# Attention and MLP on one core: first keys with 49 columns, part of the W_out split on ScalarE, one more pair rounded on GpSimd

## The chip, the cores and the metric

The kernel runs on one core of one Trainium2 chip. The metric is the device time of one execution in microseconds; the median of three runs of the kernel before is 2017.74 us (2017.72 to 2019.99). A core has TensorE (PE: matrix products; PEld is its weight load), VectorE (DVE), ScalarE (ACT), GpSimd (POOL) and SyncE (SP), which issues the loads and stores here.

## The reference

Two attentions with 49 agent vectors stand between the inputs and an MLP:

```python
a2k = softmax(scale * agents @ k.T)      # per batch: 49 x 12480, over the keys
agent_v = a2k @ v                        # 49 x 128
q2a = softmax(scale * q @ agents.T)      # 12480 x 49, over the agents
x = q2a @ agent_v                        # 12480 x 128
h = x @ w_in                             # 128 -> 2048
out = (h - tanh(h)) @ w_out              # 2048 -> 128
```

There are 4 batches, so 49,920 rows in all, everything in float32. The MLP's weights arrive as float64 and are decoded on the core from their bit patterns.

## The kernel before

**Blocks and steps.** The rows are cut into 100 blocks of 500 (the last of a batch 480). One loop in `fast` (lines 854 to 910) runs over 800 steps: a step is block `n` and one of eight pairs `i` of 128-column chunks of the 2048 hidden columns. In a step PE makes the hidden values `h` of a later step (`m1`, line 563; two steps ahead as a rule), ScalarE takes tanh and square of it (lines 573 and 578), VectorE multiplies `g = h * z` (line 583), and PE adds the pair's second product into the block's accumulator (`m2`, line 632). Two blocks form a pair of blocks with positions `pos` 0 to 15, and `w_in` is folded into the agents' values beforehand, so that `m1` multiplies the q softmax (49 wide) directly with two 49 x 2048 matrices, `awh` and `awl`.

**Two forms of the second product.** `g` is float32. In the split form GpSimd rounds it to `gh` (`high`, line 613), VectorE computes `gl = g - gh` (`low`, line 618), and PE multiplies both with W_out's rounded part `wo_h` and rest `wo_l`: six terms of two products each, 12 products. In the plain form PE multiplies `g` in float32 with `wo_f`: eight product records, and no work for GpSimd and VectorE. Positions 1, 3, 7, 8 and 9 (`PLAIN`) and all of block 0 are plain. `product` (line 828) makes `g` and, if needed, `gh`; `low(1)` in the same step makes `gl` of the step before; `out` (line 840) issues the second product of the step before.

**The start.** `phase1(0)` handles batch 0 before the loop. For each of 13 groups of eight 128-key tiles, `scores` multiplies the keys (as weights) with the agents of batches 0 and 1 side by side, 98 columns (line 273), of which the copies to SBUF (line 284) and the maxima (line 286) read only the 49 of batch 0. After each of the groups 3, 5, 7 and 9 one quarter of W_in is decoded (`load_w_in`, lines 174 to 185: one ScalarE and six VectorE instructions). `max_in` and `max_out` bring the maxima of all keys into every partition, `av` subtracts them, takes the exponential and multiplies with V (lines 344 to 380). Then come the sums, the first parts of `awh` and `awl` (line 472 to 476), and the decoding of W_out's first quarter; the other three quarters are decoded in block 0, two steps each. `split_w_out` (lines 208 to 218) makes `wo_h`, `wo_l` and `wo_f` of a quarter on GpSimd, at steps 4 and 6 (the middle quarters), 8 and 9.

**The rest.** The scores, maxima and values of batch b+1 (`phase1(b + 1)`) are jobs in a list `kq`, spread over the steps of batch b: `KS`, `VS` and `OS` say at which positions how many start (`KS`: one at position 2, two at 12). The q softmax of the next pair of blocks starts at position 2, and its scores (line 508) are issued one step on; its transposes (line 538) come at positions 11 and 15. Program order is kept on PE and GpSimd from the end of the start on, and on VectorE and ScalarE from the end of the keys on (lines 916 to 919). The order of the early loads on SP's queue is that of the list `loads` (lines 716 to 725). PSUM holds four tiles of two banks, shared by `h`, accumulators, transposes and everything else (`banks` and `misc`).

Of the kernel before, what the change touches and what calls it, by code (L numbers as in the profile page):

```python
# [12 lines left out]
F32 = mybir.dt.float32  # L13
# [11 lines left out]
A = 49  # L25
# [35 lines left out]
PLAIN = (1, 3, 7, 8, 9)  # L61
NB = dict(y=2, z=2, g=4, gh=3, gl=3)
# [40 lines left out]
class Build:  # L103
# [95 lines left out]
    def load_w_in(self, c, raw):  # L199
        tiles = (self.work.tile([128, 512], F32, tag=t, name=t, bufs=2) for t in ("de", "rem", "da", "db"))  # L200
        run(self.decode(raw, self.w_in[:, c * 512 : (c + 1) * 512], *tiles))
# [6 lines left out]
    def split_w_out(self, c):  # L208
# [4 lines left out]
        nc.gpsimd.tensor_scalar(h, w, 1.0, 0.0, ALU.mult, ALU.add)  # L213
        nc.gpsimd.tensor_tensor(l, w, h.bitcast(F32), ALU.subtract)
        nc.gpsimd.memset(self.vb[c][:, :, C : C + 1], 1.0)
        for i, t in self.wo_f.items():
            if c == i // 2:
                nc.gpsimd.tensor_scalar(t, w[:, 2 * C * (i % 2) :][:, : 2 * C], 1.0, 0.0, ALU.mult, ALU.add)

    def phase1(self, b):  # L220
# [36 lines left out]
        def scores(g):  # L257
            yield
            if g == 0:
                st["s"] = self.keep.tile([128, NG * (GT + 1) * A], F32, tag="s", name="s", bufs=1)  # L260
                if b == 0:
                    st["mxp"] = self.work.tile([128, A, 2 * NG], F32, tag="mxp", name="mxp", bufs=1)
# [7 lines left out]
            if b == 0:  # L270
                ps = self.banks("h")
                for t in range(n):
                    nc.tensor.matmul(  # L273
                        ps[:, t // 4, (t % 4) * A2 : (t % 4 + 1) * A2],
                        kt[:, t, :],
                        self.ag[:, 0:2, :],
                        start=True,
                        stop=True,
                    )
                pv = ps[:, :, : 4 * A2].rearrange("p c (t a) -> p c t a", a=A2)[:, :, :, :A]  # L280
                for c in range(-(-n // 4)):
                    m = min(4, n - 4 * c)
                    sl = slice((g * GT + 4 * c) * A, (g * GT + 4 * c + m) * A)
                    nc.scalar.copy(st["s"][:, sl].rearrange("p (t a) -> p t a", a=A), pv[:, c, :m])
                banks = -(-n // 4)
                nc.vector.tensor_reduce(
                    st["mxp"][:, :, 2 * g : 2 * g + banks].rearrange("p a c -> p c a"),
                    pv[:, :banks, : min(4, n)].rearrange("p c t a -> p c a t"),
                    axis=AX.X,
                    op=ALU.max,  # L290
                )
                if g == EARLY - 1:
                    nc.vector.tensor_reduce(
                        st["mxp"][:, :, 2 * NG - 1], st["mxp"][:, :, : 2 * EARLY], axis=AX.X, op=ALU.max
                    )
# [13 lines left out]
        def max_in():  # L309
# [3 lines left out]
            part = st["mxp"] if b else st["mxp"][:, :, 2 * EARLY :]  # L313
# [302 lines left out]
    def low(self, g, gh):  # L616
        gl = self.wtile("gl", NB["gl"])[:, : g.shape[1]].bitcast(F32R)
        self.nc.vector.tensor_tensor(gl, g, gh.bitcast(F32), ALU.subtract)  # L618
        return gl

    def m2(self, acc, i, gh, gl, wf=None):
# [7 lines left out]
        for k, (weights, g, c) in enumerate(terms):  # L629
# [55 lines left out]
    def fast(self):  # L685
# [21 lines left out]
        with ExitStack() as first:  # L707
# [15 lines left out]
            for g in range(NG):  # L723
                loads.append((self.v0, g))
# [44 lines left out]
        early = self.count()  # L769
# [5 lines left out]
        rest0 = p1[2 * NG + 3 :]  # L775
        sums = rest0.pop(0)
        q1 = q_job(1)
        next(q1)
        for _ in range(3):
            next(sums)  # L780
        next(q1)
        run(sums)
        part = rest0.pop(0)
        go(part, 3)
        go(dec[0], 3)
        run(part)
        next(q1)
        go(dec[0], 1)
        run(rest0.pop(0))
        run(dec[0])  # L790
        live = []
        kq = []
        r1, r2, done = [], [], []
# [186 lines left out]
```

## Time and profile before

| | |
|---|---|
| median of three runs | 2017.74 us |
| profiled execution: its time, its span | 2016.83 us, 2015.0 us |
| mean granted clock of TensorE | 0.997 |
| VectorE's product `g` (line 583) | 800 instructions, 1194 ns each |
| GpSimd's rounding (line 613) | 544 instructions, 1566 ns each |
| VectorE's difference (line 618) | 544 instructions, 1204 ns each |
| plain second products (line 632, from `wo_f`) | 1968 records, 578 ns each |

Times in the profile are microseconds, unless marked ns, from the span's start. A row of the timeline gives start, duration, engine, line, operation, output<-inputs, shapes and count, and in brackets the idle time of the engine before it with what ended it. A row of the windows gives, for a stretch, each engine's busy time and the number of instructions that fall into it, the granted clock of TensorE (PEclk), the mean share of the DMA engines and GB/s. A row of the groups gives count, busy time, mean of one, and idle time before. PE records of successive products overlap, since one starts while the one before it drains; the distance of their starts says more than their durations. A few per cent of the PE records are missing from the trace.

### The profile page before, as it was taken

What the parts mean: (1) busy time and instruction counts of PE and PEld (TensorE: products, weight loads), DVE (VectorE), ACT (ScalarE), POOL (GpSimd) and SP (SyncE); (2) the same over time, 40 slices, a digit from 0 to 9 for tenths busy, and PEclk for the clock granted to TensorE, in tenths of its full rate; (3) what the DMA queues carried; (4) which work ended last, traced back from release to release, by engine and by line L of the source; (5) the groups of instructions that cost most, each with busy time, mean ns of one, the idle gap of its engine ahead of it and who ended that gap; (6) DMA issues with size and microseconds to landing.
All of it is one profiled execution on the core that took longest, in us unless ns stands there. A gap on an engine that the chain in (4) does not pass through costs nothing.

```text
span 2015.0 us, 49566 instructions
## 1 busy us (share of the span) xinstructions
PE 1983.3 (98%) x20775; PEld 1464.4 (73%) x20775; DVE 1827.4 (91%) x1985; ACT 1804.1 (90%) x2044; POOL 1004.1 (50%) x709
## 2 busy tenths in 40 slices
PE   8899999999999999999999999999999999999998
PEld 7477777777677777777677777777777777777775
DVE  7899999889999998898999999889899999999997
ACT  3799989899999998899999999998999999999996
POOL 1344455555445455554454454555545546555553
PEclk9999999999999999999999999999999999999999
DMA  9322112221112222221112111221101101101100
GB/s 346 123 86 92 53 57 83 73 61 46 52 61 67 77 71 61 85 67 61 33 34 92 61 57 47 68 64 56 51 29 34 54 29 37 51 30 36 39 24 27
DMA packets 76744, 129.69 MB, mean 64 GB/s; under 512 B 5400, under 2 KB 55648, under 8 KB 76512
## 3 DMA queue, kind: packets, MB, share of 16 engines
q1 hardware_dynamic: 76512, 126.44, 19.1%
q8 instruction: 165, 2.70, 0.6%
q14 instruction: 67, 0.55, 0.1%
HBM read 81.10 MB, written 25.56 MB: 53 GB/s over the span
## 4 chain that ended last, share of the span: by engine, by line
PE 84%; ACT 9%; DVE 5%; issue 1%; DMA 0%; POOL 0%; SPq 0%; DVEq 0%; POOLq 0%
PE acc L632 49%; PE h L563 26%; ACT z L578 4%; ACT y L573 4%; DVE g L583 2%; PE misc L508 2%; PE misc L357 2%; PE pt L538 1%; PE misc L301 1%; PE h L273 1%; DVE gl L618 1%; PE misc L472 1%; ACT s L349 0%; DVE qe L524 0%; DVE s L344 0%
## 5 line engine op out<-in xcount | busy, mean ns | idle before, releaser
L613 POOL TENSOR_SCALAR gh<-g 128x1000 fp32r<-128x1000 f32 (+1 forms) x544 | 852.1, 1566 | 621.9 <-DVE g L583 578.3
L583 DVE TENSOR_TENSOR g<-h,z 128x1000 f32<-128x1000 f32 (+1 forms) x800 | 954.9, 1194 | 132.8 <-ACT z L578 121.8
L573 ACT ACTIVATE y<-h 128x1000 f32<-128x1000 f32 (+1 forms) x800 | 803.2, 1004 | 72.1 <-PE h L563 63.8
L578 ACT ACTIVATE z<-y 128x1000 f32<-128x1000 f32 (+1 forms) x800 | 831.3, 1039 | 25.4
L618 DVE TENSOR_TENSOR gl<-g,gh 128x1000 fp32r<-128x1000 f32 (+1 forms) x544 | 654.7, 1204 | 0.3
L563 PE MATMUL h<-pT,awh 49*128 49x504 f32 x1600 | 551.7, 424 | 0.0
L632 PE MATMUL acc<-g,wo_f 64*128 64x500 f32 (+1 forms) x1968 | 445.2, 578 | 0.0
L632 PE MATMUL acc<-gh,wo_l 64*128 64x500 f32 (+1 forms) x2176 | 433.0, 387 | 0.3 <-POOL gh L613 0.2
L632 PE MATMUL acc<-gh,wo_h 64*128 64x500 f32 (+1 forms) x2176 | 432.7, 386 | 0.0
L563 PE MATMUL h<-pT,awl 49*128 49x504 f32 x800 | 368.7, 461 | 10.3 <-DVE g L583 4.6
L632 PE MATMUL acc<-gl,wo_h 64*128 64x500 f32 (+1 forms) x2176 | 340.9, 387 | 1.0 <-DVE gl L618 0.5
L563 PE MATMUL h<-pb,awh 49*128 49x504 f32 x1600 | 317.4, 387 | 0.0
L563 PE MATMUL h<-pb,awl 49*128 49x504 f32 x800 | 309.0, 386 | 0.0
L632 PEld LDWEIGHTS acc<-g,wo_f 64*128 64x128 f32 x1968 | 192.6, 186 | 144.7 <-issue 126.2
L563 PEld LDWEIGHTS h<-pT,awh 49*128 49x128 f32 x1600 | 265.4, 186 | 19.5 <-issue 10.5
L632 PEld LDWEIGHTS acc<-gh,wo_h 64*128 64x128 f32 x2176 | 214.9, 186 | 36.2
L632 PEld LDWEIGHTS acc<-gl,wo_h 64*128 64x128 f32 x2176 | 212.1, 184 | 38.5 <-DVE gl L618 5.3
L632 PEld LDWEIGHTS acc<-gh,wo_l 64*128 64x128 f32 x2176 | 211.5, 184 | 37.1 <-POOL gh L613 1.1
L563 PEld LDWEIGHTS h<-pT,awl 49*128 49x128 f32 x800 | 147.4, 184 | 120.6 <-DVE o L641 49.1
L529 POOL TENSOR_TENSOR pp<-qe,pp 128x392 fp32r<-128x392 f32 x50 | 51.6, 1032 | 272.6 <-DVE pp L527 257.3
L563 PEld LDWEIGHTS h<-pb,awh 49*128 49x128 f32 x1600 | 154.6, 184 | 28.6
L563 PEld LDWEIGHTS h<-pb,awl 49*128 49x128 f32 x800 | 149.1, 186 | 12.4 <-issue 7.2
(113 smaller groups left out, 1130.0 us busy)
## 6 DMA issues: line engine op xcount, KB each, us to landing
kt<-kT SPq DMA_DIRECT2D x48, 512.0 KB
qt<-qT SPq DMA_DIRECT2D x46, 500.0 KB
outT<-o SPq DMA_DIRECT2D x46, 500.0 KB
pb<-pT SPq DMA_DIRECT2D x200, 96.5 KB
v<-v SPq DMA_DIRECT2D x36, 512.0 KB
vt<-v SPq DMA_DIRECT2D x12, 512.0 KB
raw<-w_in SPq DMA_DIRECT2D x4, 512.0 KB
v<-w_out SPq DMA_DIRECT2D x4, 512.0 KB
```

Source lines behind the costliest of these rows:

```text
L273: nc.tensor.matmul(ps[:, t // 4, (t % 4) * A2 : (t % 4 + 1) * A2], kt[:, t, :], self.ag[:, 0:2, :], start=True, stop=True,)
L301: nc.tensor.matmul(to, kt[:, t, r : r + QUART], self.ag[:, b, :], start=True, stop=True)
L357: nc.tensor.matmul(ps[HALF * odd : HALF * odd + w, : C + 1], flat[:r, t * A : t * A + w], vt[:r, t, : C + 1], start=t < 2, stop=t >= n - 2,)
L508: nc.tensor.matmul(to, qt[:, token : token + QUART], self.ag[:, b, :], start=True, stop=True)
L529: nc.gpsimd.tensor_tensor(pp[:, :, HALF:PW], ev, pp[:, :, :A].bitcast(F32), ALU.subtract)
L563: nc.tensor.matmul(h[:, c, : BT * TT], aw[a][rows[c], sl], pT[p][rows[c], :], start=k == 0, stop=k == 2)
L573: self.nc.scalar.activation(self.pair(y), h, AF.Tanh, scale=TSC)
L578: self.nc.scalar.activation(z, y, AF.Square, scale=GSC)
L583: self.nc.vector.tensor_tensor(self.pair(g), h, self.pair(z), ALU.mult)
L613: self.nc.gpsimd.tensor_scalar(gh, g, 1.0, 0.0, ALU.mult, ALU.add)
L618: self.nc.vector.tensor_tensor(gl, g, gh.bitcast(F32), ALU.subtract)
L632: nc.tensor.matmul(acc[:, r, :w], weights(c)[rows], g[rows, c * w : (c + 1) * w], start=i == 0 and k == 0, stop=i == NCH // 2 - 1 and k == ...
```

## The change

It has three parts, and some moves that go with them.

- **First keys.** The 98 moving columns become the 49 of batch 0; the scores of a group go to one bank instead of two, with one copy and a maximum over one part per group.
- **W_out and the decoding.** In the middle quarters, ScalarE makes `wo_h` and `wo_f` instead of GpSimd; `wo_l` stays on GpSimd. Three quarters of W_in are decoded between the groups of keys (after groups 3, 6 and 9) and the fourth ahead of the first product, in the place where W_out's first quarter was decoded; of that quarter's decoding, the ScalarE step and three of VectorE's come ahead of the first product, and three behind it. The loads move accordingly.
- **Pair 1.** At position 1, from block 2 on and if `kq` is empty or has scores at its head, the second product is split instead of plain, with the difference on GpSimd too. Its first eight products are issued where the plain ones were; the last four, which need `gl`, are held until the jobs of the next step have issued theirs (there, the q scores).

```diff
+POOL_LOW = (1,)
...
-        nc.gpsimd.tensor_scalar(h, w, 1.0, 0.0, ALU.mult, ALU.add)
+        if c in (1, 2):
+            nc.scalar.copy(h, w)
+        else:
+            nc.gpsimd.tensor_scalar(h, w, 1.0, 0.0, ALU.mult, ALU.add)
         nc.gpsimd.tensor_tensor(l, w, h.bitcast(F32), ALU.subtract)
...
-                nc.gpsimd.tensor_scalar(t, w[:, 2 * C * (i % 2) :][:, : 2 * C], 1.0, 0.0, ALU.mult, ALU.add)
+                on = nc.scalar.copy if c in (1, 2) else nc.gpsimd.tensor_copy
+                on(t, w[:, 2 * C * (i % 2) :][:, : 2 * C])
...
-                ps = self.banks("h")
+                ps = self.misc()[:, : n * A]
                 for t in range(n):
-                    nc.tensor.matmul(
-                        ps[:, t // 4, (t % 4) * A2 : (t % 4 + 1) * A2],
-                        kt[:, t, :],
-                        self.ag[:, 0:2, :],
...
+                    nc.tensor.matmul(ps[:, t * A : (t + 1) * A], kt[:, t, :], self.ag[:, b, :], start=True, stop=True)
+                nc.scalar.copy(st["s"][:, g * GT * A : (g * GT + n) * A], ps)
...
-    def low(self, g, gh):
+    def low(self, g, gh, pool=False):
...
-        self.nc.vector.tensor_tensor(gl, g, gh.bitcast(F32), ALU.subtract)
+        (self.nc.gpsimd if pool else self.nc.vector).tensor_tensor(gl, g, gh.bitcast(F32), ALU.subtract)
...
-    def m2(self, acc, i, gh, gl, wf=None):
+    def m2(self, acc, i, gh, gl, wf=None, part=slice(0, 6)):
...
-        for k, (weights, g, c) in enumerate(terms):
+        for k, (weights, g, c) in list(enumerate(terms))[part]:
...
-                if g % 2 == 0 and 0 < g < 10:
-                    loads.append((load_raw, g // 2 - 1))
+                if g in (2, 5, 8):
+                    loads.append((load_raw, g // 3))
                 loads.append((self.k0, g))
...
             for g in range(NG):
+                if g == 6:
+                    loads.append((load_raw, 3))
                 loads.append((self.v0, g))
...
-                if g % 2 == 1 and 2 < g < 11:
-                    self.load_w_in((g - 3) // 2, raws[(g - 3) // 2])
+                if g in (3, 6, 9):
+                    run(self.load_w_in(g // 3 - 1, raws[g // 3 - 1]))
...
+            part = rest0.pop(0)
+            go(part, 3)
+            w3 = self.load_w_in(3, raws[3])
+            go(w3, 3)
+            run(part)
+            next(q1)
+            go(w3, 1)
+            run(rest0.pop(0))
+            run(w3)
...
         go(dec[0], 3)
-        run(part)
-        next(q1)
-        go(dec[0], 1)
-        run(rest0.pop(0))
-        run(dec[0])
...
             g = self.mul(hs.pop(k), zs.pop(k), width(n))
-            plain = n == 0 or n % 2 * HP + i in PLAIN or k == len(steps) - 1
+            pos = n % 2 * HP + i
+            pool = n > 1 and pos in POOL_LOW and not (kq and kq[0][0] is not KS)
+            plain = n == 0 or pos in PLAIN and not pool or k == len(steps) - 1
             gh = None if plain else self.high(g)
-            r1.append((n, i, g, gh))
+            r1.append((n, i, g, gh, self.low(g, gh, True) if pool else None))
...
-                self.m2(acc[n], i, gh, gl, wf)
+                if gl is not None and n % 2 * HP + i in POOL_LOW:
+                    self.m2(acc[n], i, gh, gl, wf, slice(0, 4))
+                    held.append(partial(self.m2, acc[n], i, gh, gl, wf, slice(4, 6)))
+                else:
+                    self.m2(acc[n], i, gh, gl, wf)
...
             product(k)
+            if k == 0:
+                run(dec[0])
...
             self.share(False)
+            while held:
+                held.pop(0)()
             tanhs(k + 1)
```

More of the change, by code (lines that the diff above doesn't have):

```diff
@@ L200, in load_w_in @@
         tiles = (self.work.tile([128, 512], F32, tag=t, name=t, bufs=2) for t in ("de", "rem", "da", "db"))
-        run(self.decode(raw, self.w_in[:, c * 512 : (c + 1) * 512], *tiles))
+        return self.decode(raw, self.w_in[:, c * 512 : (c + 1) * 512], *tiles)
     def load_w_out(self, c, raw):
@@ L261, in scores @@
                 if b == 0:
-                    st["mxp"] = self.work.tile([128, A, 2 * NG], F32, tag="mxp", name="mxp", bufs=1)
+                    st["mxp"] = self.work.tile([128, A, NG + 1], F32, tag="mxp", name="mxp", bufs=1)
                 else:
@@ L270, in scores @@
             if b == 0:
-                ps = self.banks("h")
+                ps = self.misc()[:, : n * A]
                 for t in range(n):
-                    nc.tensor.matmul(
-                        ps[:, t // 4, (t % 4) * A2 : (t % 4 + 1) * A2],
-                        kt[:, t, :],
-                        self.ag[:, 0:2, :],
[L277 to L285, printed above, removed]
+                    nc.tensor.matmul(ps[:, t * A : (t + 1) * A], kt[:, t, :], self.ag[:, b, :], start=True, stop=True)
+                nc.scalar.copy(st["s"][:, g * GT * A : (g * GT + n) * A], ps)
                 nc.vector.tensor_reduce(
[L287 to L290, printed above, removed]
+                    st["mxp"][:, :, g], ps.rearrange("p (t a) -> p a t", a=A), axis=AX.X, op=ALU.max
                 )
                 if g == EARLY - 1:
-                    nc.vector.tensor_reduce(
-                        st["mxp"][:, :, 2 * NG - 1], st["mxp"][:, :, : 2 * EARLY], axis=AX.X, op=ALU.max
-                    )
+                    nc.vector.tensor_reduce(st["mxp"][:, :, NG], st["mxp"][:, :, :EARLY], axis=AX.X, op=ALU.max)
                 return
@@ L312, in max_in @@
             m = self.small.tile([128, A], F32, tag="m", name="m")
-            part = st["mxp"] if b else st["mxp"][:, :, 2 * EARLY :]
+            part = st["mxp"] if b else st["mxp"][:, :, EARLY:]
             nc.vector.tensor_reduce(m, part, axis=AX.X, op=ALU.max)
@@ L768, in fast @@
                 run(av[g])
-        early = self.count()
+            early = self.count()
+            rest0 = p1[2 * NG + 3 :]
+            sums = rest0.pop(0)
+            q1 = q_job(1)
+            next(q1)
+            for _ in range(3):
+                next(sums)
+            next(q1)
+            run(sums)
+            part = rest0.pop(0)
[3 more added lines that the diff above has]
+            run(part)
+            next(q1)
+            go(w3, 1)
+            run(rest0.pop(0))
+            run(w3)
         self.main = ExitStack()
@@ L774, in fast @@
         dec = [self.load_w_out(c, raws[4 + c]) for c in range(4)]
-        rest0 = p1[2 * NG + 3 :]
-        sums = rest0.pop(0)
-        q1 = q_job(1)
-        next(q1)
[L779 to L784, printed above, removed]
-        go(dec[0], 3)
-        run(part)
-        next(q1)
-        go(dec[0], 1)
-        run(rest0.pop(0))
-        run(dec[0])
+        go(dec[0], 3)
         live = []
         kq = []
-        r1, r2, done = [], [], []
+        r1, r2, done, held = [], [], [], []
         acc, outs, hs, ys, zs = {}, {}, {}, {}, {}
```

4 lines of the change are left out of this document (2 added, 2 removed).

## The prediction

> **What bounds the kernel now.** I read the page first, then the busy time by windows, then the timeline of the first 80 us, then the waits of the steady part.
>
> ```profile
> span 2015.0 us, 49566 instructions
> PE 1983.3 (98%) x20775; PEld 1464.4 (73%) x20775; DVE 1827.4 (91%) x1985; ACT 1804.1 (90%) x2044; POOL 1004.1 (50%) x709
> PE 84%; ACT 9%; DVE 5%; issue 1%; DMA 0%; POOL 0%; SPq 0%; DVEq 0%; POOLq 0%
> ```
>
> TensorE carries 84% of the chain that ended last. The steady part shows it more sharply; each window below is one pair of blocks (16 steps), the first while scores of the next batch run beside it, the second in the last batch, when nothing does.
>
> ```profile
> core 0: us, PE busy (x) PEld busy (x) DVE busy (x) ACT busy (x) POOL busy (x), PEclk, DMA share, GB/s
> 146.83:186.07 39.24, 39.24 (x542) 29.24 (x541) 36.49 (x40) 36.19 (x41) 18.85 (x14) 1.00 0.24 78
> 1673.27:1710.12 36.85, 36.85 (x350) 27.12 (x350) 33.97 (x37) 34.98 (x39) 19.62 (x14) 1.00 0.12 40
> ```
>
> PE is busy for the whole of both; VectorE and ScalarE have 2 to 3 us over, GpSimd half of the window. So in the steady part PE time saved is time saved, and work given to GpSimd is free while it is in time. The keys of batch 0, at the very start, are a stage of their own, and there the change touches PE most.
>
> **Part 1, first keys with 49 columns.** Each of the 98 tiles of keys is a 128-column weight, and 98 agent columns (two batches, of which one is used) stream past it; fp32 takes two passes, so 196 products. The change streams 49.
>
> ```profile
> 5.62 24.83 PE L273 MATMUL h<-ag,kt 128*128 128x98 f32 x196 [5.62 <-DMA kt<-kT]
> 7.31:10.72 3.41, 3.41 (x18) 3.41 (x18) 2.33 (x5) 1.23 (x3) 0.00 (x0) 1.00 0.97 360
> 14.13:17.55 3.42, 3.42 (x33) 3.42 (x32) 3.12 (x6) 0.94 (x5) 0.00 (x0) 1.00 1.03 412
> 44.13 0.94 PE L380 MATMUL h<-vt,s 128*49 128x128 f32 x14
> 51.77 0.39 PE L391 MATMUL h<-s,ones 128*128 128x49 f32 x2
> L391 PE MATMUL h<-s,ones x4: 272/275/307, 51.8 to 52.2; 128*128 128x49 f32 x2, 64*128 64x49 f32 x2
> ```
>
> The second row has 16 products of its own (two reach in from its edges), so one in 0.213 us; the third has about 30.5, so one in 0.112 us. That factor of two is the clock: the clock column reads 1.00 in both because its records begin only at 10.7, but the spacing halves there and stays so. What sets 0.112? In the L380 row two half-width products run side by side: 7 couples in 0.94 us less a tail of about 0.27 less one spacing, so 0.11 us for 128 columns, or 0.86 ns a column. At that rate 98 columns stream for 0.084 us and 49 for 0.042, both less than 0.112. The L391 row has the very shape of the change, 128-column weights and 49 columns moving: two products end 0.39 us after the first began, one lasts 0.275, so they start 0.112 apart. So the weight, not the stream, sets the rate, and halving the stream saves nothing: 0.112 at full clock, 0.213 at half.
>
> But it changes how much the array streams. Over a window of 3.41 us, 98 columns stream for 0.084 of 0.112 us (75%); 49 would stream for 0.042 of 0.112 (37%), or at half clock 0.084 of 0.213 (39%). Does the clock go by that? These windows are of the one length in which the clock column changes.
>
> ```profile
> 3.89:7.31 3.42, 1.69 (x8) 1.72 (x9) 0.37 (x3) 0.00 (x0) 0.07 (x1) 1.00 1.02 361
> 44.85:48.27 3.42, 2.14 (x39) 1.85 (x36) 3.42 (x6) 1.46 (x3) 1.12 (x1) 1.00 1.04 359
> 44.68 0.61 PE L380 MATMUL h<-vt,s 128*49 128x128 f32 x8
> 46.57 0.98 PE L538 MATMUL pt<-identr,pp 64*113 64x64 f32 x16 [1.28 <-POOL pp L529]
> 47.48 1.04 PE L380 MATMUL h<-vt,s 128*64 128x128 f32 x14
> 48.27:51.68 3.41, 3.41 (x28) 2.73 (x24) 1.97 (x4) 0.67 (x1) 0.00 (x0) 0.50 1.10 357
> 65.33:68.75 3.42, 1.74 (x12) 1.16 (x14) 3.38 (x4) 3.26 (x5) 2.73 (x5) 1.00 0.57 154
> 67.01 0.49 PE L563 MATMUL h<-pT,awl 49*128 49x504 f32 x1 [2.09 <-DVE g L583]
> 67.80 1.42 PE L632 MATMUL acc<-g,awh 64*128 64x500 f32 x6
> ```
>
> After the window 44.85:48.27 the clock is 0.50 for one window. That window streamed about 9.5 couples of L380 at 0.11 us and 8 couples of L538 of 64 columns at half that per column (one pass): 1.05 + 0.22 us, or 37%. The window 65.33:68.75 had fewer busy records (1.74 against 2.14 us) and kept its clock: there the L632 products stream without a break from 67.80 on, 0.95 us, and the three L563 couples before them for 0.63, together 46%. At the start, 3.89:7.31 streamed 8 products of 98 columns at half clock, 8 x 0.168 = 1.3 us or 39%, and the next window still ran at half clock. So streamed time orders all three, busy time does not; the border lies between 37 or 39% and 46%, and 49 columns come out on the low side, both in the clock that they start in and in the one that they would have to keep. I take it that the keys run at half clock to the end: 195 x 0.2133 + 0.5 = 42.1 us in place of 24.83, **+17.2 us**. Nothing hides it: every later step needs the maximum over all keys, and VectorE's share of this stage (below) only shrinks.
>
> Beside it: one ScalarE copy for two and a final maximum over half as many parts, worth under 0.7 us on engines that wait for PE here: 0. The loads of K lose the company of one W_in part; PE waited for K once only (the 5.62 in its row), so 0, and a slower PE asks for less.
>
> **Part 2, decoding moved.** The fourth W_in part leaves the keys' stage for the place just ahead of the first product, where the first W_out part was decoded; that one now straddles the first product (three of its VectorE steps ahead of it, three behind). The W_in part's load goes back on SP's queue past five K loads, a q load and six V loads of 0.5 MB; at the 412 GB/s of the 14.13 row that is 1.3 us each, some 15 us later, and it is needed 25 us after the keys at the earliest: 0.
>
> ```profile
> L175 DVE TENSOR_SCALAR da<-raw 128x512 uint32<-128x512 uint32 x4 | 1.7, 421 | 3.9 <-DMA raw<-w_in 3.9
> L177 DVE SCALAR_TENSOR_TENSOR da<-raw,da 128x512 uint32<-128x512 uint32 x4 | 2.8, 690 | 0.1
> L179 DVE TENSOR_SCALAR db<-da 128x512 uint32<-128x512 uint32 x4 | 1.7, 422 | 0.1
> L181 DVE SCALAR_TENSOR_TENSOR rem<-raw,db 128x512 f32<-128x512 uint32 x4 | 2.8, 689 | 0.1
> L183 DVE TENSOR_TENSOR rem<-da,rem 128x512 f32<-128x512 f32 x4 | 2.8, 689 | 0.1
> L185 DVE SCALAR_TENSOR_TENSOR w_in<-de,rem 128x512 f32<-128x512 f32 x4 | 2.7, 680 | 0.0
> 75.00:80.00 5.00, 3.54 (x22) 2.03 (x24) 4.93 (x5) 2.46 (x3) 4.20 (x7) 1.00 0.14 41
> 66.64 1.28 POOL L214 TENSOR_TENSOR wo_l<-awh,wo_h 128x512 fp32r<-128x512 f32 x1
> 66.87 1.38 DVE L175 TENSOR_SCALAR gh<-v 128x512 uint32<-128x512 uint32 x1
> 77.23 1.43 DVE L179 TENSOR_SCALAR gh<-gh 128x512 uint32<-128x512 uint32 x1
> ```
>
> One decode is 3.6 us of VectorE. Under the keys it was covered; between 53 and 80 us VectorE is the bound (4.93 of 5.00 us busy, PE 3.54), so it adds **+3.6**. Against it stands part 3: GpSimd's split of W_out collides with decoding there: L175 took 1.38 us beside L214 where it takes 0.42, L179 1.43. With two of four roundings on ScalarE (2.46 of 5.00 busy, so its three copies of 0.3 to 0.7 us cost nothing) and tied to ScalarE's order, most of that work falls behind the last decode; what stays is about one collision. GpSimd now waits for ScalarE's copy, with the other quarters and a q difference queued behind; the split weights are first read in step 10, some 10 us later, so I count nothing for that. I credit **-2.5** (bounds 0 and -3.6). Sum +1.1, from 0 to +3.6.
>
> **Part 4, pair 1 on GpSimd.** It applies from pair 1 of blocks on where the next batch's job list is empty or has scores at its head. Thirteen groups of scores at three per pair hold it in pairs 1-4, 13-16 and 25-29; the list is empty from pair 38 to 49: 25 cases.
>
> ```profile
> 149.01 1.37 PE acc L632 x12
> 153.33 1.68 PE acc L632 x8
> L517 POOL TENSOR_TENSOR qe<-qe,qm 128x392 f32<-128x392 f32 x50 | 43.0, 860 | 32.4 <-DVE qm L515 32.3
> L214 POOL TENSOR_TENSOR wo_l<-awh,wo_h 128x512 fp32r<-128x512 f32 x4 | 5.4, 1354 | 0.3
> 1680.05 1.03 POOL L613 TENSOR_SCALAR gh<-g 128x1000 fp32r<-128x1000 f32 x1 [3.59 <-DVE g L583]
> 1685.30 1.20 DVE L583 TENSOR_TENSOR g<-h,z 128x1000 f32<-128x1000 f32 x1 [1.35 <-ACT z L578]
> ```
>
> Twelve split products take 1.37 us, eight plain ones 1.68: 0.31 saved a case, at most -7.8. GpSimd gets one rounding (1.03 us alone) and one difference of 1000 elements: 2.2 us at L517's rate per element, 2.6 at L214's. Together 3.2 to 3.6, up to 0.8 more where VectorE's difference is in the way, into the 3.59 us that GpSimd idles before its next rounding (the 1680.05 row). The overrun of up to 0.9 us is passed to VectorE's next difference and product, and used up in the 1.35 us that VectorE waits for ScalarE three steps on. The held products come behind the q scores, about 1.7 us after the first eight, which is what the difference needs. I take **-6.5** (0.26 a case); the ends are -7.8 and +2.5 (0.1 lost a case, if PSUM comes free late).
>
> **Sum.** The profiled execution took 2016.83 us; 2016.83 + 17.2 + 1.1 - 6.5 = 2028.6. It lies 0.9 under the median of the three runs (2017.74), so the forecast is **2029.5 us**. Its own range: 16 to 18, 0 to 3.6, -7.8 to +2.5 give 2026 to 2042 at the outside; with not more than one of them at its bad end, 2026 to 2034.
>
> **Rivals.**
> - *The clock rises all the same* (other side). For: the products follow each other without a gap, with weights loading all the time. Against: the three windows. Then the keys stay at 24.8 us, and 2017.74 + 1.1 - 6.5 = 2012, between 2009 and 2018. It decides at the streamed share: if the border is under 39% for the way up, faster. [...]
> - *The weight isn't the limit*: keys then go at VectorE's pace, about 4 us less than now: 2008. Against: the L391 row.
> - *GpSimd comes late*: the held products wait, PE loses 0.3 where it should gain, 25 x 0.3 = +7.5: 2017.74 + 17.2 + 1.1 + 7.5 = 2043. For: the 3.59 us gap is filled to the brim.
> - *The clock rises midway*, say after 20 of 42 us: the gains and the loss nearly cancel, 2018 to 2022.
>
> **Numbers.** Forecast 0.65, clock rises 0.20, weight not the limit 0.05, GpSimd late 0.06, midway 0.04. A measurement can tell 0.2% (4 us). Faster 0.25, same 0.04, slower 0.71. The range 2010 to 2034 takes in the forecast's own and most of the first rival.
>
> **What would show it.** Right: the first keys' 196 products spread over 42 us at a spacing of 0.213, the stage of the maxima near 48 us instead of 31; pairs 38 to 49 at 36.5 us each instead of 36.85; the wo_f products down by 25 x 8. Wrong: spacing 0.112 after 10 us (the first rival), or pairs 38 to 49 no shorter, with PE waiting for GpSimd's difference.

## The result and the profile after

The kernel after takes 2038.36 us in the median of four runs (2037.85 to 2041.42), the kernel before, run beside it, 2018.05 us. The ratio is 1.0103, with a 95% interval of 1.009 to 1.0116: slower by about 21 us. The direction was forecast, the size was not: 2029.5 was expected, at most 2034.

The page of after, its heads and its chain by engine:

```profile
span 2036.2 us, 49820 instructions
PE 2000.8 (98%) x20875; PEld 1481.4 (73%) x20875; DVE 1832.3 (90%) x1985; ACT 1804.0 (89%) x2035; POOL 1104.0 (54%) x756
PE 81%; ACT 9%; DVE 7%; issue 1%; DMA 1%; POOL 0%; DVEq 0%; SPq 0%; ACTq 0%
```

PE is still busy for 98% of the span. GpSimd has 100 us of work more, and VectorE's share of the chain rose from 5% to 7%, a first sign that PE waits for it somewhere.

The first place to look is the keys. Here are the key products and the final maximum from the timeline of after, and two stretches of its windows (the columns are those of the windows of before):

```profile
5.81 42.02 PE L278 MATMUL misc<-ag,kt 128*128 128x49 f32 x196 [5.81 <-DMA kt<-kT]
48.44 0.31 DVE L303 TENSOR_REDUCE m<-mxp 128x49 f32<-128x147 f32 x1
...
7.28:10.69 3.41, 3.41 (x18) 3.41 (x18) 2.25 (x5) 1.17 (x2) 0.00 (x0) 1.00 0.99 375
20.00:30.00 10.00, 10.00 (x49) 10.00 (x48) 5.05 (x9) 1.78 (x5) 0.00 (x0) 1.00 0.71 241
30.00:47.80 17.80, 17.80 (x84) 17.67 (x83) 3.82 (x7) 2.87 (x6) 0.00 (x0) 1.00 0.58 174
```

The 196 products take 42.02 us where they took 24.83. Between 20 and 30 us the window has 49 of them, or one in about 0.21 us, and so it stays up to 47.8. The clock column is of no use here, since its first record at full clock comes at 56.16 us (at 10.72 in before) and it reads 1.00 until the records begin; the spacing is the evidence. VectorE is busy for 3.82 of the last 17.8 us, so it is PE that sets this stage, and nothing hides the loss.

The second place is GpSimd. These are the groups of after for its new difference, and for VectorE's difference:

```profile
L607 POOL TENSOR_TENSOR gl<-g,gh 128x1000 fp32r<-128x1000 f32 x25 | 59.0, 2359 | 2.1
...
L607 DVE TENSOR_TENSOR gl<-g,gh 128x1000 fp32r<-128x1000 f32 (+1 forms) x544 | 657.9, 1209 | 22.6 <-POOL gh L602 22.4
...
L621 PE MATMUL acc<-g,wo_f 64*128 64x500 f32 (+1 forms) x1768 | 398.9, 578 | 0.0
```

25 differences of 2.36 us went to GpSimd, and the plain records fell from 1968 to 1768, by 25 times 8, as they should. But VectorE's difference, which waits on GpSimd's rounding, now idles 22.4 us for it: 0.9 us a case.

To see where the rest of the time went, the span is cut at the VectorE product `g` that opens each pair of blocks. The sums are differences to the profile of before, in us. Each row is one profile, and kernels with the same start as before (e3, e4, e7, e8, e11 to e13) differ from it by +0.1 to +0.9 us in the first column, so tenths there mean little:

| kernel | up to the first product | 13 pairs with pair 1 beside scores | pairs 38 to 48 | everything else | span |
|---|---|---|---|---|---|
| after | +18.5 | +0.6 | +2.8 | -0.8 | +21.2 |
| keys alone (e1) | +17.5 | +0.4 | 0.0 | -0.3 | +17.6 |
| after without its keys (e2) | +0.8 | -0.9 | +2.8 | -0.7 | +2.0 |
| pair 1 alone, 25 cases (e3) | +0.1 | -0.7 | +2.8 | -0.8 | +1.4 |

The keys are worth +17.5. The pairs of the last batch, forecast to fall by 0.26 us each, rose by 0.25; the 13 beside the scores, forecast to fall by 3.4 in all, fell by 0.7 in e3 and rose by 0.6 in after. That is where the forecast and the result part.

### The profile page after: what moved, and what is told of

It reads as the page before. It is cut to its first block, busy times and chain, and to the rows that moved or that the text cites. A ratio compares the mean times of both kernels' runs of the same rounds, so it can differ in the third digit from the quotient of the medians.

```text
span 2036.2 us, 49820 instructions
## 1 busy us (share of the span) xinstructions
PE 2000.8 (98%) x20875; PEld 1481.4 (73%) x20875; DVE 1832.3 (90%) x1985; ACT 1804.0 (89%) x2035; POOL 1104.0 (54%) x756
## 4 chain that ended last, share of the span: by engine, by line
PE 81%; ACT 9%; DVE 7%; issue 1%; DMA 1%; POOL 0%; DVEq 0%; SPq 0%; ACTq 0%
PE acc L621 46%; PE h L552 25%; ACT z L567 4%; ACT y L562 4%; DVE g L572 4%; PE misc L278 2%; PE misc L497 2%; PE misc L346 2%; PE pt L527 1%; PE misc L290 1%; DVE gl L607 1%; PE misc L461 1%; ACT s L338 0%; DVE qe L513 0%; DVE qs L510 0%
## 5 line engine op out<-in xcount | busy, mean ns | idle before, releaser
L602 POOL TENSOR_SCALAR gh<-g 128x1000 fp32r<-128x1000 f32 (+1 forms) x569 | 897.0, 1577 | 519.7 <-DVE g L572 456.3
L572 DVE TENSOR_TENSOR g<-h,z 128x1000 f32<-128x1000 f32 (+1 forms) x800 | 955.5, 1195 | 111.1 <-ACT z L567 98.4
L607 DVE TENSOR_TENSOR gl<-g,gh 128x1000 fp32r<-128x1000 f32 (+1 forms) x544 | 657.9, 1209 | 22.6 <-POOL gh L602 22.4
L621 PE MATMUL acc<-gh,wo_l 64*128 64x500 f32 (+1 forms) x2276 | 451.1, 387 | 0.3
L621 PE MATMUL acc<-gh,wo_h 64*128 64x500 f32 (+1 forms) x2276 | 450.8, 386 | 0.0
L621 PE MATMUL acc<-g,wo_f 64*128 64x500 f32 (+1 forms) x1768 | 398.9, 578 | 0.0
L621 PE MATMUL acc<-gl,wo_h 64*128 64x500 f32 (+1 forms) x2276 | 358.9, 389 | 2.2 <-issue 0.9
L621 PEld LDWEIGHTS acc<-g,wo_f 64*128 64x128 f32 x1768 | 171.7, 186 | 133.2 <-issue 115.8
L621 PEld LDWEIGHTS acc<-gh,wo_h 64*128 64x128 f32 x2276 | 223.2, 186 | 39.9
L621 PEld LDWEIGHTS acc<-gl,wo_h 64*128 64x128 f32 x2276 | 218.0, 184 | 44.6 <-DVE gl L607 6.1
L621 PEld LDWEIGHTS acc<-gh,wo_l 64*128 64x128 f32 x2276 | 219.8, 184 | 40.5 <-POOL gh L602 1.1
```

The lines of the kernel that those rows point to most:

```text
L572: self.nc.vector.tensor_tensor(self.pair(g), h, self.pair(z), ALU.mult)
L602: self.nc.gpsimd.tensor_scalar(gh, g, 1.0, 0.0, ALU.mult, ALU.add)
L607: (self.nc.gpsimd if pool else self.nc.vector).tensor_tensor(gl, g, gh.bitcast(F32), ALU.subtract)
L621: nc.tensor.matmul(acc[:, r, :w], weights(c)[rows], g[rows, c * w : (c + 1) * w], start=i == 0 and k == 0, stop=i == NCH // 2 - 1 and k == ...
```

## The experiments

### The keys

**e1_keys49**: the kernel before with the part on the keys alone; its core is this (the copies and maxima follow it).

```diff
-                        self.ag[:, 0:2, :],
...
+                    nc.tensor.matmul(ps[:, t * A : (t + 1) * A], kt[:, t, :], self.ag[:, b, :], start=True, stop=True)
```

> The kernel before with the 49 columns alone (its four W_in parts still decoded between the keys, pair 1 plain). Clock theory: the 196 products stay at a spacing of 0.213 us, the keys take 42 us instead of 24.8, the kernel is 17 to 17.5 us slower than before (about 2035). Rival 'the weight sets the pace at full clock, the loss comes from the moved decoding': spacing 0.112 after the first 5 us and the time of before within 1 us (2018). Rival 'one PSUM bank and one copy cost': the keys between 25 and 30 us, 1 to 5 us slower.

Measured: 2034.03 us against 2017.89, ratio 1.0082 (1.0067 to 1.0098). In the profile the products take the same 42 us as in after, and the maximum over all keys comes 17 us late (48.43 for 31.38). By the times the keys alone lose 16.5 us (13.5 to 19.8), by the profile 17.6 of the span: the +17.2 fits both.

**e2_keys98**: the kernel after, with the 98 columns put back.

> The changed kernel with the 98 columns, two banks and two copies of before back: what is left of the change is the decoding, the split on ScalarE and pair 1. Clock theory: 17.4 us come back, 2038.4 - 17.4 = 2021, 1 to 4 us slower than before. If the change's loss lay elsewhere: 2030 or more. If pair 1 gained what was forecast (6.5 us) it would be 2012, faster than before.

Measured: 2019.77, ratio 1.001 (1.0001 to 1.0019). Without the keys the rest of the change is no gain but a small loss.

**e5_cols60** and **e6_cols70**: the kernel before, with 60 or 70 of its 98 columns streamed; the rest of the columns of batch 1 is left out (nothing reads it).

```diff
-                        ps[:, t // 4, (t % 4) * A2 : (t % 4 + 1) * A2],
+                        ps[:, t // 4, (t % 4) * A2 : (t % 4) * A2 + 60],
...
-                        self.ag[:, 0:2, :],
+                        self.ag.rearrange("p b a -> p (b a)")[:, :60],
```

> The kernel before, but 60 columns stream past each tile of keys (49 of batch 0 and 11 of batch 1) instead of 98. Clock theory: at half clock 60 columns stream for 0.103 of each 0.213 us (48%), between the 39% at which the clock stayed low and the 46% at which a window kept it; if the border for rising is the same as for falling, the clock rises and the keys take 25 us; if it is higher than 48% they take 42. Rival 'not the streamed share but the number of batches, banks or copies': as 98 columns, 25 us, whatever the count.

> As the run with 60 columns, with 70: 0.120 of 0.213 us at half clock, 56% streamed. Clock theory: the clock rises as with 98 (77%), the keys take 25 us, time of before, since the weights set 0.112 us in both. If it stays low, the border for rising lies between 56 and 77% and the kernel is 16 to 17 us slower.

Measured, one time each: 2033.83 and 2035.25 us, against 2017.55. The key products in their timelines, of 60 columns and of 70:

```profile
5.92 42.04 PE L273 MATMUL h<-ag,kt 128*128 128x60 f32 x196 [5.92 <-DMA kt<-kT]
```

```profile
6.15 42.06 PE L273 MATMUL h<-ag,kt 128*128 128x70 f32 x196 [6.15 <-DMA kt<-kT]
```

Both stay at half clock to the end; for 70 columns the expectation was that the clock rises. Estimated at 1.72 ns a column at half clock, twice the 0.86 of the prediction, 60 columns fill 0.103 of the 0.213 us between two products (48%), 70 fill 0.120 (56%) and 98 fill 0.168 (79%, not the 77% of the expectation). Only the last brings the clock up. By this estimate the border for rising lies between 56% and 79%, above the 37% at which a window of before lost the full clock and the 46% at which one kept it. And 49, 60 and 70 columns all take 42.0 us: the weight sets the spacing, not the stream.

**e9_quarter**: the kernel before with 49 columns, and each weight cut into four of 32 columns, which batches 1 to 3 do already (the copies and maxima are those of e1).

```diff
-                    nc.tensor.matmul(
-                        ps[:, t // 4, (t % 4) * A2 : (t % 4 + 1) * A2],
-                        kt[:, t, :],
-                        self.ag[:, 0:2, :],
+                    for r in range(0, 128, QUART):
+                        to = ps[r : r + QUART, t * A : (t + 1) * A]
+                        nc.tensor.matmul(to, kt[:, t, r : r + QUART], self.ag[:, b, :], start=True, stop=True)
```

> The kernel before, with only the first keys changed: 49 agent columns, and each 128-column weight cut into four of 32 columns that write to four quarters of the partitions, the form that batches 1 to 3 have. Theory (the 128-column weight load sets the rate, and the clock follows the streamed share): 64 products of the small form end 0.90 us after the first began in the batch 0 q scores of the kernel before, about 0.010 us each, so 784 take about 8 us at full clock and 16 at half; PE is no longer the bound of the stage, VectorE is (21.25 of 23.63 us busy from 8.17 on, with the same maxima and decodings), so the maxima end at 29.5 to 31.8 where they ended at 31.74, and the time is 2015.5 to 2018 against 2017.9 of before. The stream is gapless at first, so the clock rises in the first 15 us as before; it may fall once PE runs out of loaded keys (8 us of work in 20 us is 40%, between the 37% that lost it and the 46% that kept it). Rival (49 columns keep the clock low by their number, however the weights are cut): no full-clock record before 30 us, the same end of the maxima, and then the softmax and the first V products at half clock for one or two windows, 2019 to 2022.

Measured: 2022.78 against 2017.12, ratio 1.003 (1.002 to 1.004). Neither theory gave that. Short products are quickly done and then PE waits, and the clock goes with it. The windows of this kernel, cut about the length in which the clock changes:

```profile
14.00:17.40 3.40, 2.64 (x127) 2.48 (x120) 3.18 (x6) 1.44 (x3) 0.00 (x0) 1.00 1.03 414
17.40:20.80 3.40, 0.14 (x13) 0.01 (x2) 3.33 (x8) 1.04 (x2) 0.00 (x0) 0.98 1.02 402
20.80:24.20 3.40, 2.73 (x127) 2.64 (x127) 3.30 (x6) 1.43 (x3) 0.00 (x0) 0.52 1.03 412
24.20:27.60 3.40, 0.06 (x7) 0.00 (x0) 2.90 (x6) 0.12 (x1) 0.00 (x0) 0.98 1.03 400
27.60:31.00 3.40, 2.84 (x127) 2.65 (x127) 0.92 (x2) 0.97 (x2) 0.00 (x0) 0.51 0.68 229
31.00:34.40 3.40, 1.60 (x127) 1.47 (x127) 1.35 (x3) 0.97 (x2) 0.00 (x0) 1.00 0.80 257
```

This is the clearest picture of the clock in the case. Read PE's busy time (second column) against the clock of the next row. After a window with 0.14 us of work the clock is 0.52, after one with 2.73 it is 0.98, after 0.06 it is 0.51, after 2.84 it is 1.00. (The first row's own 1.00 is no measurement, since the records begin at 17.25; its 127 products take about as long as those at half clock.) Each burst of work meets the clock that the pause before it has earned; in the last row the same 127 products take 1.60 us, against 2.73 and 2.84 at half clock. The maximum over the keys comes at 38.84 us (31.38 in before). Ahead of these products PE idles 8.1 us for loads of K, and 13.6 us in five pauses for which the waits name nothing. The trace has more on those five: each ends 2.3 to 2.5 us after a transfer of 16 KB on the DMA queue q8, whose kind is "instruction", has begun (at 11.38, 19.13, 25.27, 29.62 and 34.59 us), and from each to the next lie 127 products. So it seems that PE waits there for the next part of its program, which grows with the number of products. No run tested this; the run shows the clock's behaviour and not the best that quartered keys could give.

### The decoding and the split of W_out

**e_decode** has only the hunks of the moved decoding and the ScalarE split; **e_decode_nosplit** the same without this part:

```diff
-        nc.gpsimd.tensor_scalar(h, w, 1.0, 0.0, ALU.mult, ALU.add)
+        if c in (1, 2):
+            nc.scalar.copy(h, w)
+        else:
+            nc.gpsimd.tensor_scalar(h, w, 1.0, 0.0, ALU.mult, ALU.add)
...
-                nc.gpsimd.tensor_scalar(t, w[:, 2 * C * (i % 2) :][:, : 2 * C], 1.0, 0.0, ALU.mult, ALU.add)
+                on = nc.scalar.copy if c in (1, 2) else nc.gpsimd.tensor_copy
+                on(t, w[:, 2 * C * (i % 2) :][:, : 2 * C])
```

> The kernel before with only the moved decoding and the ScalarE split of W_out's middle quarters (parts 2 and 3). The prediction had +3.6 for the decoding and -2.5 for the split: +1.1, 2019.0 against 2017.9. Rival (the moved decoding finds gaps in VectorE that the windows hide, and the split is worth nothing): +1.0 here and the same without the split.

> The kernel before with only the moved decoding (part 2 alone, all of W_out split by GpSimd). The prediction's sizes give +3.6, 2021.5 against 2017.9; the rival (the decoding costs 1 and the split is worth nothing) gives 2019. If the first product stands more than 2 us later than with the ScalarE split, the split earns its credit.

Measured: 2019.55 and 2020.31 against 2017.12, ratios 1.0013 (1.0004 to 1.0022) and 1.0012 (1.0002 to 1.0021). Both cost about 2.5 us, 0.4 to 4.4 by the intervals, and the split makes no difference that the times can tell. In the profiles it is there and small. Up to the first product, which stands ahead of all splitting, the two are 1.7 and 1.0 us behind before, a difference within the scatter named above; the first pair of blocks, where the splitting is, is then 0.3 us longer with ScalarE's help and 1.9 without it. A decoding step of that pair shows why, first without ScalarE's split, then with it:

```profile
69.75 1.38 DVE L175 TENSOR_SCALAR gh<-v 128x512 uint32<-128x512 uint32 x1
```

```profile
70.41 0.42 DVE L175 TENSOR_SCALAR gh<-v 128x512 uint32<-128x512 uint32 x1
```

Without ScalarE's split, GpSimd's difference `wo_l` runs beside this step (69.51 to 70.79 us); with it, GpSimd has no work there. A collision that cost VectorE 0.96 us is gone, as forecast. In all, the split is worth about 1.6 us of the pair (1.9 less 0.3) where 2.5 were credited.

### Pair 1 on GpSimd

**e3_pair1**: the kernel before with the pair 1 part alone, in its 25 cases.

> The kernel before with pair 1 on GpSimd alone, in all 25 cases. From the trace of the change: gain of 0.3 us in most of the 13 pairs beside the scores (-3.9), loss of 0.25 in each of 11 pairs of the last batch (+2.8), so about -1 without the single pauses that the change's trace has in pairs 4, 13, 26 and 28 (+4 together); with them +2. Forecast of before: -6.5 (2011.5).

Measured: 2019.15 against 2017.89, ratio 1.0007 (0.9998 to 1.0016). The part that was to bring -6.5 brings no gain.

**e4_pair1_ks**: the same, but only in the 13 cases beside scores.

```diff
-            pool = n > 1 and pos in POOL_LOW and not (kq and kq[0][0] is not KS)
+            pool = n > 1 and pos in POOL_LOW and bool(kq) and kq[0][0] is KS
```

> As the run with pair 1 alone, but only beside the scores of the next batch (pairs 1-4, 13-16, 25-29); pairs 38 to 49 stay plain. If the last batch is where it loses (GpSimd's difference pushes its next rounding, and through VectorE the release of a PSUM tile): 2.5 to 3 us faster than the run with all 25, 3 to 4 us faster than before if the pauses in the middle don't come back, near the time of before if they do. If the loss lies in the scores' pairs: no faster than the run with all 25.

Measured: 2015.21 against 2017.89, ratio 0.9989 (0.998 to 0.9998): a small gain, about 2 us, and 3.9 us less than with all 25 cases. So the loss lies in the last batch. (In its profile the 13 pairs themselves give only 0.1 of 1.7 us. The rest lies behind the start of the last pair, where e4 does the work of before; e9, with pair 1 plain, is as short there, so this part is not shown to come from pair 1.) One of its pairs as a window, first in after, then in e4, where pair 1 is plain there as in before:

```profile
1656.50:1693.62 37.12, 36.85 (x354) 27.14 (x354) 34.35 (x36) 34.92 (x39) 23.91 (x16) 1.00 0.12 40
```

```profile
1636.45:1673.36 36.91, 36.91 (x350) 27.66 (x350) 34.00 (x36) 35.02 (x39) 19.60 (x14) 1.00 0.12 40
```

In after PE idles 0.27 us of the pair, and its busy time (whose ends are modelled) has hardly shrunk, though its products should take 0.31 less; so the whole length is the better measure. The place is seen in the timeline of after, 3.6 to 11.3 us into the next pair:

```profile
1697.21 1.82 POOL L602 TENSOR_SCALAR gh<-g 128x1000 fp32r<-128x1000 f32 x1 [0.40 <-PE acc L621]
...
1699.12 2.36 POOL L607 TENSOR_TENSOR gl<-g,gh 128x1000 fp32r<-128x1000 f32 x1
...
1701.44 1.05 POOL L602 TENSOR_SCALAR gh<-g 128x1000 fp32r<-128x1000 f32 x1
...
1702.52 1.20 DVE L607 TENSOR_TENSOR gl<-g,gh 128x1000 fp32r<-128x1000 f32 x1 [0.89 <-POOL gh L602]
...
1703.63 1.19 DVE L572 TENSOR_TENSOR g<-h,z 128x1000 f32<-128x1000 f32 x1
...
1704.88 0.49 PE L552 MATMUL h<-pT,awl 49*128 49x504 f32 x1 [0.32 <-DVE g L572]
```

Read it as a relay. GpSimd rounds pair 1 (1.82 us, beside VectorE's difference), then makes its difference (2.36), and only then rounds pair 2. VectorE waits 0.89 us for that rounding, makes its difference, and behind it in its queue stands the product `g` of a later step. That product frees the PSUM tile which PE's next `h` needs, and PE waits.

The waits of the last batch say the same in sums (us in all, times, longest), first in before, then in after:

```profile
DVE g L583 <- ACT z L578: 24.6, 33, 1.4
...
PEld h L563 <- DVE g L583: 6.0, 22, 0.3
```

```profile
PEld h L552 <- DVE g L572: 13.9, 33, 0.7
...
DVE g L572 <- ACT z L567: 11.6, 33, 0.7
...
PE h L552 <- DVE g L572: 3.2, 11, 0.3
```

VectorE does use up its waits for ScalarE, 11.6 us where it had 24.6. But the weight loads for `h` wait for its product 13.9 us in place of 6.0, and PE's products 3.2 in place of none. VectorE's own instructions are hardly longer than in before (1205 ns for 1190 the difference, 1197 for 1195 the product, in pairs 38 to 48), so it comes late and is not slowed by GpSimd's work beside it.

The next runs try this theory from other sides. **e7_vec** leaves the rounding on GpSimd and gives pair 1's difference to VectorE.

```diff
-            r1.append((n, i, g, gh, self.low(g, gh, True) if pool else None))
+            r1.append((n, i, g, gh, None))
```

> Pair 1 split in the same 25 cases and with its last four products held, but the difference is made by VectorE as for every other pair; GpSimd only rounds. If GpSimd's 2.4 us difference in front of its next rounding is what turns the last batch's gain into a loss: pairs 38 to 49 go at 36.5 to 36.6 us instead of 37.1, and the time is 4 to 8 us under that of pair 1 on GpSimd (2011 to 2015). If VectorE has no room for 1.2 us more (it was busy 34 of 36.9 us), pairs stay at 37 us or more and the time is 2018 or more.

Measured: 2016.84 against 2017.55, ratio 0.9996 (0.9987 to 1.0005); the pairs 38 to 48 take 36.97 us in the mean, between 36.88 in before and 37.13 in after, and so neither of the two values expected. VectorE no longer waits for GpSimd, but it has 1.2 us more in front of the same product `g`, and the weight loads for `h` wait for that product as long as in after: 14.0 us over these pairs.

**e8_late** keeps the difference on GpSimd, but queues it behind the rounding of pair 2, and holds the last four products one step longer.

```diff
-            r1.append((n, i, g, gh, self.low(g, gh, True) if pool else None))
+            if waiting:
+                late = waiting.pop()
+                r1[-1] = r1[-1][:4] + (self.low(*late, True),)
+            r1.append((n, i, g, gh, None))
+            if pool:
+                waiting.append((g, gh))
...
+                    held.append((k + 2, partial(self.m2, acc[n], i, gh, gl, wf, slice(4, 6))))
...
+            while held and held[0][0] <= k:
+                held.pop(0)[1]()
```

> Pair 1 on GpSimd in all 25 cases, but its difference is queued behind the rounding of pair 2 instead of ahead of it, and the last four products wait one step more. If the place in GpSimd's queue is the cause: pair 2's rounding is on time again, VectorE waits for it no longer, pairs 38 to 49 at 36.5 to 36.6 us, 4 to 8 us under the run with pair 1 alone (2011 to 2015). If GpSimd just has too much to do, or the split form itself saves nothing: 37 us a pair as before the shift.

Measured: 2043.47 against 2017.55, ratio 1.0131 (1.0115 to 1.0146). The expectation failed badly: the pairs are longer, by some 0.65 us beside scores and by 1.36 in the last batch. The timeline of e8:

```profile
1694.64 1.05 POOL L614 TENSOR_SCALAR gh<-g 128x1000 fp32r<-128x1000 f32 x1 [1.40 <-DVE g L584]
...
1695.64 2.36 POOL L619 TENSOR_TENSOR gl<-g,gh 128x1000 fp32r<-128x1000 f32 x1
1695.77 3.29 DVE L619 TENSOR_TENSOR gl<-g,gh 128x1000 fp32r<-128x1000 f32 x1
...
1699.11 1.18 PE L633 MATMUL acc<-gl,wo_h 64*128 64x500 f32 x8 [1.24 <-DVE gl L619]
```

The rounding of pair 2 is early now, but VectorE's difference falls beside GpSimd's and takes 3.29 us instead of 1.2: it ends 1.1 us after GpSimd's has ended, as if it had stood still until then. The 3.29 us are the 2.23 that GpSimd's still has to go when it starts, and 1.06 more. The mended order removed one wait and made a worse one, so it could not decide on the theory.

**e11_idle_full** and **e12_idle_round** put GpSimd's work alone into the kernel before: rounding and difference of pair 1, or the rounding alone, are made in the same 25 cases and not used. The products of pair 1 stay plain.

The core of e11, which e12 has without its second line:

```diff
+            if pool:
+                self.low(g, gh, True)
+                gh = None
             r1.append((n, i, g, gh, None))
```

> The kernel before, plus GpSimd's rounding and difference of pair 1 in the same 25 cases, written to their buffers and not used: the products of pair 1 stay the eight plain ones. TensorE's work is that of before; only GpSimd's extra 3.4 us a case is added. Theory (the loss of the last batch is GpSimd's overrun, passed by way of the next rounding and VectorE's next difference to the release of a PSUM tile): the split pair saved 0.31 and still cost 0.25 in the last batch, so the stall is about 0.55 a pair, and here, without the saving, pairs 38 to 48 go from 36.88 to 37.4, 2023 to 2026 in all against 2017.5. Rival (the stall comes from the order of the products: eight ahead, four held behind other work, PSUM held longer): the pairs stay at 36.9, 2017 to 2019.

> As the unused full one, but with GpSimd's rounding alone (1.03 us a case), no difference. The GpSimd overrun theory: 1.03 us fits into the 3.59 us that GpSimd idles, so the last batch stays at 36.9 a pair and the time at 2017 to 2018.5. [...]

Measured: 2022.20 and 2018.18 against 2017.60, ratios 1.0022 (1.0012 to 1.0032) and 1.0003 (0.9994 to 1.0013). Pairs 38 to 48 take 37.22 and 36.87 us, against 36.88. The waits of VectorE's difference in the last batch, in e11 (in us in all, times, longest):

```profile
DVE gl L619 <- POOL gh L614: 9.8, 10, 1.0
```

GpSimd's work by itself, with PE's products untouched, makes VectorE wait 1.0 us a pair and the pair 0.34 us longer. The chain that ended last runs over PE alone in these pairs of before; in e11 GpSimd's rounding and difference have 14% of it. The rounding alone does nothing, and leaves the waits of the weight loads for `h` at the 6.0 us of before. That rules out the order of the products as the main cause. The pair is shorter than the 37.4 us expected, and that explains the size: in e11 PE has 0.31 us more to do than in after, but its pair is only 0.09 longer, which is what VectorE waits longer (0.98 for 0.89). The end of the relay sets a time before which PE cannot go on, and what PE saves ahead of that time is waited away.

**e13_half**: the kernel before with pair 1 split in all 25 cases, with GpSimd's difference cut to 500 of the 1000 elements and VectorE doing the other half.

```diff
+        if gl is None:
+            gl = self.wtile("gl", NB["gl"])[:, : g.shape[1]].bitcast(F32R)
+            sl = slice(0, g.shape[1] // 2 if pool else g.shape[1])
+        else:
+            sl = slice(g.shape[1] // 2, g.shape[1])
+        on = self.nc.gpsimd if pool else self.nc.vector
+        on.tensor_tensor(gl[:, sl], g[:, sl], gh[:, sl].bitcast(F32), ALU.subtract)
```

> Pair 1 split in the same 25 cases, with GpSimd's difference cut to the first 500 of its 1000 elements (about 1.2 us in place of 2.36) and VectorE taking the other 500 (0.6 us) ahead of the next difference. GpSimd overrun theory: GpSimd is done 1.2 us earlier, which is more than the 0.89 that VectorE waited, and VectorE loses 0.6 of its slack: pairs 38 to 48 at 36.6 to 36.8, 2012 to 2015 in all. Rival (whatever is added to VectorE or GpSimd in this place comes back as a late PSUM tile, as with the difference on VectorE alone, 36.97): 36.95 to 37.1, 2016 to 2019.

Measured: 2011.60 against 2017.60, ratio 0.9969 (0.9957 to 0.998), faster than both kernels. A pair of the last batch as a window, and the relay in its timeline:

```profile
1635.84:1672.41 36.57, 36.57 (x354) 27.28 (x354) 34.56 (x37) 34.87 (x39) 23.10 (x16) 1.00 0.12 40
```

```profile
1641.34 1.27 POOL L624 TENSOR_TENSOR gl<-g,gh 128x500 fp32r<-128x500 f32 x1
...
1642.38 0.77 DVE L624 TENSOR_TENSOR gl<-g,gh 128x500 fp32r<-128x500 f32 x1
1642.62 1.42 POOL L614 TENSOR_SCALAR gh<-g 128x1000 fp32r<-128x1000 f32 x1
...
1644.18 1.18 DVE L624 TENSOR_TENSOR gl<-g,gh 128x1000 fp32r<-128x1000 f32 x1
```

GpSimd is through with its half in 1.27 us, the rounding of pair 2 ends at 1644.04, and VectorE's next difference starts at 1644.18 without a wait. The pairs 38 to 48 take 36.57 us in the mean, 0.30 less than in before: almost the whole 0.31 that the split products save. The weight loads for `h` wait 6.9 us there, near the 6.0 of before, and the chain runs over PE alone again. This is the forecast's own saving, in the last batch, once GpSimd's overrun is gone. Of the 4.7 us that this profile gains, 3.3 lie there.

**e10_best** joins the quartered keys of e9 with pair 1 of e4.

> The kernel before with pair 1 on GpSimd beside the scores only (13 cases; alone it gave 2015.21 against 2017.89), and the first keys quartered with 49 columns. If the two add up: 2015.2 less what the quartered keys give, 0 to 2 us: 2013 to 2015.5, faster than both kernels. If the quartered keys cost the clock (the rival above), 2016.5 to 2019.

Measured: 2021.04 against 2017.12, ratio 1.002 (1.0011 to 1.0029): what the quartered keys lose stays lost.

## Why the prediction was right and wrong

**Part 1, the keys: right.** 42.1 us were forecast at a spacing of 0.2133 and 42.02 measured; the 196 products, the late maximum (48.44 where "near 48" was said) and the loss (+17.2, in e1 +17.5 up to the first product) are those of the text. The steps to it held as well: halving the stream did not speed up the products, and it kept the clock from rising. e5 and e6 add that the rival "the clock rises all the same" was further off than its 0.20 says: even 56% of streamed time doesn't raise it.

**Parts 2 and 3: the sum fits, the terms look smaller.** +3.6 and -2.5 were forecast, +1.1 in all. The decoding without the split costs 2.9 us up to the end of the first pair (1.0 + 1.9) and 2.4 by the times (0.4 to 4.2); with it 2.0 (1.7 + 0.3), by the times 2.6 (0.8 to 4.4); beside pair 1 the two add 0.6 to the span (e2 less e3). The credit shows 1.6 us in the first pair instead of 2.5; the cost of 2.9 instead of 3.6 is within the scatter of these profiles, and within the interval of the times. So the sum lies among the values measured, but if both terms are smaller, its fit is partly luck.

**Part 4, pair 1: wrong, and this made the miss.** -6.5 was forecast and e3 gave +1.4 in its profile, 7.9 of the 8.9 us between 2029.5 and 2038.36. Not every step failed. The saving on PE is there: 0.30 of the forecast 0.31 (e13). GpSimd's times are those of the text: 2.36 us for the difference, between 2.2 and 2.6, and 1.82 for the rounding, 0.8 more than alone. Even the overrun of "up to 0.9 us" is the 0.89 that VectorE waits. The step that failed is the next one: the overrun "is passed to VectorE's next difference and product, and used up in the 1.35 us that VectorE waits for ScalarE three steps on". It was priced by VectorE's own slack, and VectorE does use that up. But the late product frees a PSUM tile, and PE wants it before those three steps are over; there PE has no slack. The waits of before had a hint: PE's weight load for `h` waits on VectorE's `g` in the last batch already, 6.0 us in 22 times. In e3's profile the pairs 38 to 48 are 5.7 of the 7.9 us, and the 13 pairs beside the scores 2.7; other places gave 0.5 back.

Beside the scores VectorE waits as well (22.4 us in the 25 cases), yet eight of the 13 pairs fell there, by 0.3 to 1.2 us. Four of them rose, by 0.35 to 2.0, with pauses of PE like this one in the timeline of after:

```profile
253.61 0.28 PE L290 MATMUL misc<-ag,kt 128*32 128x49 f32 x3 [1.40 <-issue]
```

The waits name nothing that PE waits for here. Such pauses are in before too, in other pairs, and change place when the program changes. In e2, e3, e4 and e13 nearly the same pairs rise. Of the 13 x 0.31 = 4.0 us that these pairs should save, 0.7 is left in e3 and nothing in after. The DMA records of the traces point at a source: all 33 pauses of PE of this kind that last 0.3 us or more behind the first pair, in the 17 profiles, end 2.2 to 2.7 us after an "instruction" transfer on queue q8 has begun, and in after these transfers come only every 11.7 us in the mean of pairs 1 to 37 (9.6 in the 13 pairs beside the scores). So PE seems to wait for its own program, as in e9; no run tested it. It is not all: in pair 26 PE also waits 0.62 us for VectorE's `g`, with no such transfer near, and that stays open.

**The range: too narrow by its own terms.** The bad end of part 4 was given as +2.5. Put into the sum alone, it makes 2038.5, almost what was measured. But the text went on with "not more than one of them at its bad end, 2026 to 2034", which that one term already breaks. The bound was seen, with its reason, a PSUM tile that comes free late, and not carried through. The rival "GpSimd late", at 0.06, had GpSimd's lateness right, but not the wait: the held products wait for GpSimd's difference once in after, 0.5 us, and what PE waits for is the tile of the next `h`.

## What to carry to other kernels

When work is moved to an idle engine, follow what waits on that engine's next result down to the engine that sets the end, and compare the delay with the smallest slack on that path. If the moved piece is too long, cut it: half of it on each engine gained 6 us here, where the whole of it on either gained nothing clear of the noise. And before the work of PE is made smaller at the start of a kernel, ask whether the rest still streams enough to get the clock up (here 98 columns a weight did, 70 did not).

## What the runs showed of the hardware that was not expected

- By the estimate above, the granted clock has a higher border for rising than for falling in this kernel: 56% of streamed time (70 columns of fp32 per 128-column weight) doesn't raise it, 79% does, while at full clock 37% lost it and 46% kept it. e9 shows the same with one form of product: 1.94 us of work from 10.43 to 13.84 us, at half clock by its pace, did not raise the clock, and 1.60 us from 30.90 to 34.32, at full clock, kept it. In e1, e5 and e6, PE's records fill all of the 10 us between 20 and 30 us, as they do in after, and the clock stays low for the 42 us of the keys; so a full share of records in flight does not raise it here.
- Two differences of 1000 elements, VectorE's and GpSimd's, at the same time cost VectorE 3.29 us in place of 1.2, while GpSimd's 2.36 stays 2.36 (e8, at 1695.77 us).
- PE's pauses without a named cause, 0.3 to 1.7 us in the loop and up to 3.9 us in e9, end 2.2 to 2.7 us after an "instruction" transfer of 16 KB has begun (33 of 33 in the loop, 5 of 5 in e9). That PE waits for its program there is likely and was not tested.
